# Expert steps of a fused attention and mixture-of-experts kernel: scatters behind the scaling, row loads ahead of the transposing transfers, another order in the first three steps

## The chip, the cores and the metric

The kernel runs on one core of one Trainium2 chip. The metric is the time of one execution on the device in microseconds (us); the kernel before has three timed runs, and one more execution was taken by the hardware profiler. Five engines work beside each other, each on its own list of instructions in the order of that list: PE (matmul), ACT (activations), DVE (vector), POOL (GpSimd) and SP, which only issues transfers. An engine that waits for one instruction starts none behind it.

## The reference

```python
def phi(x):                                   # x: q or k, scaled, [8, 8, 576, 64]
    proj = np.einsum('bhsd,md->bhsm', x, omega)
    h = proj - np.sum(x * x, -1, keepdims=True) / 2.0
    return np.exp(h - np.max(h, -1, keepdims=True)) / np.sqrt(m)
kv, z = einsum('bhsm,bhsd->bhmd', k_p, v), np.sum(k_p, axis=2)
num, den = einsum('bhsm,bhmd->bhsd', q_p, kv), einsum('bhsm,bhm->bhs', q_p, z) + 1e-06
x = (num / den).transpose(0, 2, 1, 3).reshape(4608, 512)
...
logits = xn @ en.T / tau                      # rows and expert embeddings, normalised
expert_idx = np.argmax(logits, axis=1)        # one of 8 experts for each token
gate_w = softmax(logits)[arange, expert_idx]
for e in range(8):
    mask = expert_idx == e
    h = np.maximum(x[mask] @ w1[e], 0.0)      # w1[e]: 512 x 1024
    out[mask] = gate_w[mask, None] * (h @ w2[e])   # w2[e]: 1024 x 512
```

Everything is float32. A product is made of three matmuls of parts rounded to fp32r (high by high, high by low, low by high).

## The kernel before

**Stages.** The attention runs over 36 tiles of 128 tokens and writes each token's 512 numbers, its logits and its number (a row of 521 floats) into a table `xs` in device memory, sorted by expert, with an indirect transfer. A small plan on DVE then says which 128 rows of `xs` and which quarter of which expert's weights each expert step takes. `NSTAT = 38` steps are written out; two of them (0 and 1) are worked off inside the attention, and the loop `for t in range(NPRE, NSTAT)` (L993, `NPRE = 2`) writes out steps 2 to 37.

**A step.** Step t takes 128 rows of `xs` (`xg[t]`, loaded by `x_of`, L852), multiplies them by the up weights w1 of its expert in two halves `pa` of 512 columns (24 matmuls of 128x128 by 128x512), applies the relu, turns the hidden words so that they can be the next stationary operand, multiplies by the down weights w2 (`down`, 24 matmuls into `nu`), scales with the gate (`scaled`, L247, DVE) and scatters the rows to `y` (`store`, L270, an indirect transfer that POOL issues). From step 5 on (`SHIFT = 5`) the down product at step t is that of u = t - 2, before that of u = t - 1. So the PE's list has 48 matmuls of 512 columns in each step of the steady part.

**Turning.** In the first steps `x_turned` and `h_turned` (L855, L877) transpose on PE. Otherwise the upper and lower 16 bits of each word go into two planes `pl` (`apart16`, L907: one plane by ACT, one by DVE), two transposing transfers on SP write `t16` (`turned16`, L912, shown as `t<-pl`), and `rejoin` (L924) puts the words `wd` together again; `summed` (L939) then makes the high parts (`xh`, `hh`, on ACT) and the low parts (`xl`, `hl`, on DVE). From `XPE = 9` on the rows of step t + 2 go through the same planes at step t, and the planes have one buffer each.

**Weights.** Step t uses a weight buffer of two halves of four quarters. `weights` (L988) loads 512 KB of one quarter into `raww1` or `raww2` (two buffers each) on SP, `split` (L897) rounds it: the first four quarters by ACT (high, L202) and DVE or POOL (low, L204), the later ones by DVE (high, L206) and POOL (low, L207). Steps 2 and 3 use a half that was filled during the attention; the matmuls of step t from 4 on wait for both parts of quarter t - 1.

**Loads of rows.** `xload` (L158) ties a load to earlier ones: up to t = 4 to the writes into `xs` (among them eight writes of padding, `pad`), later to the landing of the load before it (`last_x`). `ring` holds six buffers, so that the load for step t + 3 also waits until the scatter of step t - 3 has read its buffer.

All five engines' lists from L920 on stand as the code writes them (`manual_schedule`).

## Time and profile before

| | |
|---|---|
| median of three runs | 676.94 us (673.33 to 677.71) |
| the profiled execution | 671.0 us, of which the span of its instructions is 669.4 us |
| PE busy | 646.7 us (97%) |
| weight loads of PE | 541.1 us (81%) |
| DVE busy | 497.5 us (74%) |
| ACT busy | 416.0 us (62%) |
| POOL busy | 330.7 us (49%) |
| mean device memory traffic | 158 GB/s over the span |

The expert steps begin at about 247 us of the span and end with the last scatter at 662 us. A row of a timeline says at which us of the span an instruction starts, how many us it takes, its engine, its line, what it writes and reads (buffer numbers left out), and in brackets how long its engine sat idle before it and what ended that. A PE row's duration is longer than its share of the engine, since matmuls overlap: the distance from one start to the next counts. SP's rows (SPq) show the issue of a transfer, not its flight.

### The profile page before, as it was taken

How to read it: one execution, taken by the hardware profiler on the slowest of the kernel's cores; microseconds unless marked ns; L12 is line 12 of the kernel's file. 1: busy time of each engine (PE TensorE's matmuls, PEld its weight loads, DVE VectorE, ACT ScalarE, POOL GpSimd, SP SyncE). 2: the span in 40 equal slices, each digit the busy share in tenths (PEclk: the TensorE clock that was granted, in tenths of full speed). 3: DMA queues.
4: the chain of work that ended last, by engine and by line, in shares of the span. 5: the costliest groups of instructions: out<-in, count | busy, mean ns of one | idle time of the engine just before them, and what ended most of it. 6: DMA issues, size and time to landing. Idle time of an engine off the chain costs nothing. (4 is left out here: it accounts for less than half of the span.)

```text
span 669.4 us, 18009 instructions
## 1 busy us (share of the span) xinstructions
PE 646.7 (97%) x6051; PEld 541.1 (81%) x6052; DVE 497.5 (74%) x952; ACT 416.0 (62%) x1074; POOL 330.7 (49%) x414
## 2 busy tenths in 40 slices
PE   8999999999989998999999999999999999999993
PEld 7899999999877787788788778888888888888882
DVE  4688888899888745586878777777777777777871
ACT  6888898898886517553747465656565556565530
POOL 2013333435887544545555454655554655465553
PEclk9999999999999999999999999999999999999998
DMA  7546556569862268869887888787888787979721
GB/s 244 175 145 191 169 196 212 169 209 293 259 193 98 82 214 292 236 142 205 214 237 186 195 226 211 218 198 216 207 220 226 204 214 212 229 198 213 199 89 43
DMA packets 142346, 131.85 MB, mean 197 GB/s; under 512 B 106728, under 2 KB 106856, under 8 KB 142258
## 3 DMA queue, kind: packets, MB, share of 16 engines
q1 hardware_dynamic: 135794, 110.04, 61.3%
q0 software_dynamic: 6320, 20.38, 8.6%
q8 instruction: 55, 0.90, 0.6%
q10 hardware_dynamic: 144, 0.26, 0.1%
q14 instruction: 33, 0.27, 0.1%
HBM read 83.78 MB, written 21.97 MB: 158 GB/s over the span
## 5 line engine op out<-in xcount | busy, mean ns | idle before, releaser
L207 POOL TENSOR_TENSOR w1l<-raww,w1h 128x1024 f32 x34 | 89.8, 2641 | 164.4 <-DVE w1h L206 139.0
L241 PE MATMUL nu<-w2h,hl 128*128 (+1 forms) x288 | 113.7, 395 | 1.6 <-DVE hl L948 1.6
L241 PE MATMUL nu<-w2h,hh 128*128 (+1 forms) x288 | 113.8, 395 | 0.0
L241 PE MATMUL nu<-w2l,hh 128*128 (+1 forms) x288 | 113.6, 394 | 0.0
L241 PE MATMUL pa<-w1h,xl 128*128 (+1 forms) x280 | 111.1, 397 | 0.9 <-DVE xl L947 0.7
L241 PE MATMUL pa<-w1h,xh 128*128 (+1 forms) x280 | 110.8, 396 | 0.0
L241 PE MATMUL pa<-w1l,xh 128*128 (+1 forms) x280 | 110.5, 395 | 0.0
L905 DVE TENSOR_REDUCE wd<-t 128x1024 uint16<-128x1024 uint16 x68 | 90.0, 1323 | 3.4 <-DMA t<-pl 3.3
L338 ACT ACTIVATE ftk<-pjk,nmk 128x128 f32<-128x128 f32 x288 | 83.8, 415 | 5.7 <-DVE nmk L331 5.4
L338 ACT ACTIVATE ftq<-pjq,nmq 128x128 f32<-128x128 f32 x288 | 79.5, 418 | 9.5 <-DVE nmq L331 9.4
L909 ACT ACTIVATE pl<-pa 128x512 uint16<-128x512 uint16 x68 | 39.5, 586 | 72.2 <-DMA t<-pl 70.5
L905 DVE TENSOR_REDUCE pl<-pa 128x512 uint16<-128x512 uint16 x68 | 46.7, 690 | 49.7 <-ACT pl L909 49.6
L207 POOL TENSOR_TENSOR w2l<-raww,w2h 128x1024 f32 x34 | 83.0, 2442 | 0.0
L327 PE MATMUL pjq<-om,qt 64*128 64x128 f32 x576 | 76.2, 285 | 1.5 <-ACT ftk L338 1.0
L327 PE MATMUL pjk<-om,kt 64*128 64x128 f32 x576 | 76.3, 284 | 1.2 <-DVE om L600 1.2
L944 ACT ACTIVATE hh<-wd 128x1024 fp32r<-128x1024 f32 x34 | 36.1, 1061 | 59.9 <-DVE wd L905 52.5
L327 PEld LDWEIGHTS pjk<-om,kt 64*128 64x128 f32 x576 | 63.7, 187 | 8.7 <-issue 4.8
L241 PEld LDWEIGHTS nu<-w2h,hl 128*128 128x128 f32 x288 | 54.2, 188 | 14.7 <-DVE hl L948 2.1
L327 PEld LDWEIGHTS pjq<-om,qt 64*128 64x128 f32 x576 | 63.7, 187 | 2.8 <-ACT ftk L338 1.2
L241 PEld LDWEIGHTS pa<-w1h,xl 128*128 128x128 f32 x280 | 52.7, 188 | 15.1 <-DVE xl L947 2.9
L241 PEld LDWEIGHTS nu<-w2h,hh 128*128 128x128 f32 x288 | 54.3, 188 | 12.7
L241 PEld LDWEIGHTS nu<-w2l,hh 128*128 128x128 f32 x288 | 54.3, 188 | 12.5
(311 smaller groups left out, 1251.7 us busy)
## 6 DMA issues: line engine op xcount, KB each, us to landing
raww<-w1q SPq DMA_DIRECT2D x38, 512.0 KB, 4.1
raww<-w2q SPq DMA_DIRECT2D x38, 512.0 KB, 5.1
qt<-qT SPq DMA_DIRECT2D x36, 256.0 KB, 4.1
kt<-kT SPq DMA_DIRECT2D x35, 256.0 KB, 3.4
xgp<-xs SPq DMA_DIRECT2D x20, 260.5 KB, 3.1
xg<-xs SPq DMA_DIRECT2D x18, 260.5 KB, 3.2
rf<-w1q SPq DMA_DIRECT2D x4, 512.0 KB
rf<-w2q SPq DMA_DIRECT2D x4, 512.0 KB, 6.3
```

The source lines that it names most:

```text
L207: il = nc.gpsimd.tensor_tensor(at(l, dp), raw, at(h, dp).bitcast(F32), op=ALU.subtract)
L241: done.append(nc.tensor.matmul(dst, x[:, c * P : (c + 1) * P], ws.rearrange("p o f -> p (o f)"), start=(begin and i == 0 and k == 0), stop ...
L327: nc.tensor.matmul(st["pj" + w, i, a][:, c, :], st[w, i][r, c, :], om[r, :], start=True, stop=True)
L338: nc.scalar.activation(ft[:, h, :], pj[:, h, :], AF.Exp, bias=nm[:, h : h + 1])
L905: nc.vector.tensor_reduce(to, src.unsqueeze(2), axis=AX.X, op=ALU.max)
L909: nc.scalar.activation(planes[1][:, o : o + 512], halved(src)[:, :, 1], AF.Copy)
L944: nc.scalar.activation(hh, wd[:, 0:F], AF.Relu)
```

## The change

The change reorders; it adds and removes no work. In the loop over the steps:

- `store` follows each `scaled` at once, where it stood behind the two weight splits of the step.
- The load of the rows of step t + 3 (`rows_of`) stands ahead of the two transposing transfers of step t, where it stood at the step's end. Steps 2 and 5 keep it at the end.
- In the first three steps: the first two quarters of w1 are loaded ahead of those of w2; the load of step 4's rows goes ahead of the loads of w1's quarters 2 and 3; `h_turned` for step 2 stands in the middle of step 3's products; the splits of quarters 0 to 3 of w1 and w2 stand later in the lists; in step 4 `hl` is made ahead of the split of quarter 4.
- In step 5 the split of w1 stands ahead of the norms.

```diff
--- before.py
+++ after.py
@@ -884,15 +884,15 @@
     xg, xt, hid, raws, po = {}, {}, {}, {}, {}
     xg[NPRE] = xgp[NPRE]
     xg[NPRE + 1] = x_of(NPRE + 1, reg("row", NPRE + 1))
-    for t in range(NPRE):
-        for wn in W:
+    for wn in W:
+        for t in range(NPRE):
             raws[wn, t] = wload(wn, t, reg("wsrc", t))
     for e in range(PADP, E):
         pad(e)
     got.append(x2)
+    xg[NPRE + 2] = x_of(NPRE + 2, reg("row", NPRE + 2))
     raws["w1", NPRE] = wload("w1", NPRE, reg("wsrc", NPRE))
     raws["w1", NPRE + 1] = wload("w1", NPRE + 1, reg("wsrc", NPRE + 1))
-    xg[NPRE + 2] = x_of(NPRE + 2, reg("row", NPRE + 2))
 
     def split(wn, t):
         if t < NSTAT:
@@ -989,6 +989,10 @@
             if NPRE <= t < NSTAT and (wn, t) not in raws:
                 raws[wn, t] = wload(wn, t, reg("wsrc", t))
 
+        def rows_of(t):
+            if t < NSTAT and t not in xg:
+                xg[t] = x_of(t, reg("row", t))
+
         low, high, both = range(4), range(4, 8), range(8)
         for t in range(NPRE, NSTAT):
             u = t - 1 if t < SHIFT else t - 2
@@ -996,10 +1000,8 @@
             near = t in (NPRE, ends)
             if t > NPRE + 1:
                 weights("w1", t + 1)
-            if t > NPRE + 1:
+            if t > NPRE + 2:
                 weights("w2", u + 1)
-            elif t == NPRE:
-                weights("w2", t)
             late = (t - 1) in turn
             early = late and (t < SHIFT or t == ends)
             if early:
@@ -1012,6 +1014,8 @@
                     scaled(po.pop(v), xg[v], gates[v])
                     store(v, xg[v])
 
+            if t == SHIFT:
+                split("w1", t)
             if t == SHIFT - 1 or t > SHIFT and t % 3 == 0:
                 roots_of(batch(t)[0])
             elif t == SHIFT or t > SHIFT and t % 3 == 1:
@@ -1020,23 +1024,27 @@
             elif t > SHIFT:
                 inverted(totals[batch(t)[0] - 1])
             if t > SHIFT:
-                for v in po:
-                    scaled(po[v], xg[v], gates[v])
-            if t != NPRE + 1:
-                split("w1", t if t > NPRE else 0)
+                for v in list(po):
+                    scaled(po.pop(v), xg[v], gates[v])
+                    store(v, xg[v])
+            if early and t < SHIFT:
+                next(sm)
+            if t > NPRE + 1 and t != SHIFT:
+                split("w1", t)
             if t > SHIFT:
                 split("w2", u)
-                for v in list(po):
-                    po.pop(v)
-                    store(v, xg[v])
-            if early:
+            if early and t > SHIFT:
                 next(sm)
+            if t == NPRE + 2:
+                split("w2", NPRE)
             planes = None if near else [p2.tile([P, F + DM], U16, name=f"pl{t}_{k}", tag=f"pl{k}", bufs=1) for k in range(2)]
             par = reg("par", t) if t >= NQ else 0
             pa = [bank(f"pa{t}_{a}", ("px", "py")[a], 2) for a in range(2)]
             computed("w1", t, products(pa[0], xt[t], "w1", par, low, 0, True, True))
             if t == NPRE or NPRE + 1 < t < XPE - 1:
                 xt[t + 1] = x_turned(t + 1, xg[t + 1])
+            if t == NPRE + 1:
+                hid[t - 1] = h_turned(t - 1, h)
             if near:
                 h = words(t)
                 nc.scalar.activation(h[:, 0:512], pa[0], AF.Relu)
@@ -1055,7 +1063,11 @@
                 nc.scalar.activation(h[:, 512:F], pa[1], AF.Relu)
             else:
                 apart16(pa[1], planes, 512)
+                if t != SHIFT:
+                    rows_of(t + 3)
                 turn[t] = turned16(t, planes, F + DM if far else F)
+            if t == NPRE + 2:
+                weights("w2", u + 1)
             if late and not early:
                 rejoin(t - 1, wn[0], 0, F, 1)
             if t == SHIFT:
@@ -1068,19 +1080,19 @@
                 next(sm)
                 next(sm)
             if t == NPRE:
+                split("w1", 0)
                 split("w1", 1)
-                hid[t] = h_turned(t, h)
-                split("w2", 0)
-                split("w2", 1)
-                split("w1", t)
             elif t == NPRE + 1:
                 weights("w1", t + 1)
+                split("w1", NPRE)
                 split("w1", t)
                 down(u, low)
                 xt[t + 1] = x_turned(t + 1, xg[t + 1])
-                split("w2", u)
+                split("w2", 0)
+                split("w2", 1)
                 down(u, high)
-                weights("w2", u + 1)
+                weights("w2", NPRE)
+                weights("w2", t)
             elif t != SHIFT:
                 down(u, both)
             if t == NPRE + 1:
@@ -1089,8 +1101,7 @@
                 squares_of(NPRE + 3, NPRE + 4)
             elif NPRE + 2 < t < NSTAT - 2:
                 squares_of(t + 2)
-            if t + 3 < NSTAT:
-                xg[t + 3] = x_of(t + 3, reg("row", t + 3))
+            rows_of(t + 3)
         weights("w2", ends)
         split("w2", ends - 1)
         hid[ends] = h_turned(ends, h)
```

The first place is SP's list at the head of the expert steps. `raww_2` and `raww_3` with `w1q` are quarters 2 and 3 of w1; `xg_5122`, `xg_5123` and `xgp_103` are the rows of steps 4, 5 and 6; `t_3_0` and `t_3_1` are the transposing transfers of step 3. Before:

```order
L175 ISA
L175 DMA raww_2_5207<-w1q 128x1024
L175 ISA
L175 DMA raww_3_5209<-w1q 128x1024
L159 ISA
L159 DMA xg_5122<-xs 128x521
L175 ISA
L175 DMA raww_2_5214<-w2q 128x1024
L159 ISA
L159 DMA xg_5123<-xs 128x521
L916 DMA_TRANSPOSE t_3_0_5313<-pl_0_5281 128x8x128
L916 DMA_TRANSPOSE t_3_1_5315<-pl_1_5282 128x8x128
```

And of the change, in the same place, right behind the last write of padding:

```order
L159 ISA
L159 DMA xg_5122<-xs 128x521
L175 ISA
L175 DMA raww_2_5208<-w1q 128x1024
L175 ISA
L175 DMA raww_3_5210<-w1q 128x1024
L159 ISA
L159 DMA xg_5123<-xs 128x521
L159 ISA
L159 DMA xgp_103<-xs 128x521
L916 DMA_TRANSPOSE t_3_0_5306<-pl_0_5257 128x8x128
L916 DMA_TRANSPOSE t_3_1_5308<-pl_1_5258 128x8x128
```

The rows of step 4 moved ahead of the two weight quarters, the rows of step 6 moved from behind the transposing transfers to ahead of them, and the load of quarter 2 of w2 moved away behind them.

The second place is ACT's list at step 2. `raww_0` and `raww_1` are quarters of w1, `pt` and `ph` are transposes on PE, `wd` is the hidden words of step 2. Before:

```order
L202 ACTIVATE w1h<-raww_0_5191 128x1024
L228 ACTIVATE xh_5232<-pt_5234 128x512
L1042 ACTIVATE wd_5241<-pa_0_5218 128x512
L1055 ACTIVATE wd_5241<-pa_1_5219 128x512
L202 ACTIVATE w1h<-raww_1_5195 128x1024
L228 ACTIVATE hh_5258<-ph_0_5260 128x512
L228 ACTIVATE hh_5258<-ph_1_5267 128x512
```

And of the change:

```order
L228 ACTIVATE xh_5228<-pt_5230 128x512
L1050 ACTIVATE wd_5237<-pa_0_5214 128x512
L1063 ACTIVATE wd_5237<-pa_1_5215 128x512
L202 ACTIVATE w1h<-raww_0_5191 128x1024
L202 ACTIVATE w1h<-raww_1_5193 128x1024
L228 ACTIVATE hh_5273<-ph_0_5275 128x512
L228 ACTIVATE hh_5273<-ph_1_5282 128x512
```

The rounding of quarter 0 moved from ahead of the three activations of step 2 to behind them.

The third place is POOL's list at step 7, as in every step of the steady part: the low parts of one quarter of w1 and of w2, and the scatter to `y`. Before:

```order
L207 ISA
L207 TENSOR_TENSOR w1l<-raww_7_5639,w1h 128x1024
L207 ISA
L207 TENSOR_TENSOR w2l<-raww_5_5641,w2h 128x1024
L271 DMA y<-xg_5122 4608x512
```

And of the change:

```order
L271 DMA y<-xg_5122 4608x512
L207 ISA
L207 TENSOR_TENSOR w1l<-raww_7_5639,w1h 128x1024
L207 ISA
L207 TENSOR_TENSOR w2l<-raww_5_5641,w2h 128x1024
```

The scatter moved from behind the two low parts to ahead of them.

## Rows read from the trace of the kernel before

**Rows 1.** Busy time (instructions) by engine, granted clock, DMA share, GB/s; steady part
```profile
412.00:640.00 228.00, 228.00 (x982) 184.38 (x981) 174.49 (x254) 129.03 (x237) 121.73 (x61) 1.00 0.82 211
```

**Rows 2.** Timeline, PE: start, us, engine, line, operation, tiles, idle before; steps 2 to 5
```profile
254.98 1.15 PE L227 MATMUL ph<-ident,wd 128*128 128x128 f32 x8 [1.71 <-ACT wd L1042]
...
267.55 0.40 PE L241 MATMUL pa<-w1h,xh 128*128 x1
...
273.57 0.39 PE L241 MATMUL nu<-w2h,hh 128*128 128x512 f32 x1
...
275.85 0.50 PE L241 MATMUL nu<-w2h,hl 128*128 128x512 f32 x1 [1.65 <-DVE hl L948]
```

**Rows 3.** Timeline, PE, at the start of step 9
```profile
322.80 0.51 PE L241 MATMUL pa<-w1h,xl 128*128 x1 [0.73 <-DVE xl L947]
```

**Rows 4.** Waits from 240 us on: who, for whom, us in total, times, longest
```profile
ACT pl L909 <- DMA xg<-xs: 12.2, 14, 2.1
...
PEld pa L241 <- DVE xl L947: 2.9, 6, 1.2
```

**Rows 5.** Timeline, ACT, step 2
```profile
252.89 1.06 ACT L202 ACTIVATE w1h<-raww 128x1024 fp32r<-128x1024 f32 x1 [8.32 <-DMA raww<-w1q]
```

**Rows 6.** Timeline, DVE, steps 2 to 4
```profile
253.98 1.22 DVE L204 TENSOR_TENSOR w1l<-raww,w1h 128x1024 fp32r<-128x1024 f32 x1 [5.84 <-ACT w1h L202]
...
270.97 1.32 DVE L905 TENSOR_REDUCE wd<-t 128x1024 uint16<-128x1024 uint16 x1 [1.10 <-DMA t<-pl]
...
273.97 0.69 DVE L206 CAST w1h<-raww 128x1024 f32 x1 [1.67 <-DMA raww<-w1q]
274.58 1.22 DVE L948 SCALAR_TENSOR_TENSOR hl<-wd,hh 128x1024 fp32r<-128x1024 f32 x1
```

**Rows 7.** Timeline, SP (issues of transfers), steps 2 to 4
```profile
255.23 4.34 SPq L175 DMA_DIRECT2D raww<-w1q  x2
259.96 0.33 SPq L159 DMA_DIRECT2D xg<-xs  x1
...
264.68 2.76 SPq L916 DMA_TRANSPOSE t<-pl  x2
```

**Rows 8.** Line L175 at 248.3 us (quarter 1 of w2): issue to landing
```profile
DMA to landing us min/median/max: 9.8/9.8/9.8
```

**Rows 9.** Line L159 at 239.7 us (rows of step 2, alone): issue to landing
```profile
DMA to landing us min/median/max: 2.7/2.7/2.7
```

**Rows 10.** Line L175 at 259.2 us (quarter 3 of w1, alone): issue to landing
```profile
DMA to landing us min/median/max: 3.3/3.3/3.3
```

**Rows 11.** Line L916, step 3 (second transposing transfer): issue to landing
```profile
DMA to landing us min/median/max: 4.8/4.8/4.8
```

**Rows 12.** Line L916, 300 to 640 us (61 transposing transfers): issue to landing
```profile
DMA to landing us min/median/max: 3.7/4.1/6.2
```

**Rows 13.** Page, costliest groups: count, busy us, mean ns
```profile
L207 POOL TENSOR_TENSOR w1l<-raww,w1h 128x1024 f32 x34 | 89.8, 2641 | 164.4 <-DVE w1h L206 139.0
...
L207 POOL TENSOR_TENSOR w2l<-raww,w2h 128x1024 f32 x34 | 83.0, 2442 | 0.0
```

**Rows 14.** Timeline of all engines, one step of the steady part
```profile
404.11 0.74 DVE L248 TENSOR_SCALAR xgp<-nu,totalb 128x512 f32<-128x512 f32 x1
...
410.23 0.69 DVE L905 TENSOR_REDUCE pl<-pa 128x512 uint16<-128x512 uint16 x1 [0.49 <-ACT pl L909]
...
412.05 0.73 DVE L947 TENSOR_TENSOR xl<-wd,xh 128x512 fp32r<-128x512 f32 x1
412.06 0.99 POOL L271 DMA_INDIRECT y<-xgp  x1 [0.16 <-issue]
```

**Rows 15.** Line L271, 300 to 640 us (30 scatters): issue to landing
```profile
DMA to landing us min/median/max: 2.7/3.6/6.8
```

**Rows 16.** Timeline of all engines, step 6: a scatter beside a cast
```profile
292.44 1.08 POOL L271 DMA_INDIRECT y<-xg  x1 [0.30 <-issue]
...
292.58 0.69 DVE L206 CAST w1h<-raww 128x1024 f32 x1
```

## Prediction

> **What bounds the kernel now.** I read the busy times by stage first, to see who is never idle. In the steady part PE is busy in all of its 228 us, at the full granted clock, so a matmul costs 228.00 / 982 = 0.232 us [rows 1], and 48 of them make a step of 11.15 us. Nothing that only makes another engine faster or idle can shorten that part. So I asked the PE timeline for its idle places, and there are few in the expert steps. At 254.98 PE has waited 1.71 us for the hidden words of step 2; at 275.85 it has waited 1.65 us for `hl` of step 3 [rows 2]; at 322.80 it has lost 0.73 us to `xl` [rows 3]. PE's durations overlap, so such a number hides some 0.17 us of idle time each (a matmul shows about 0.40 and advances 0.232). For the short waits at other step starts the weight loads are the finer instrument: they waited for `xl` six times, 2.9 us in all [rows 4]. All that this change can win by removing waits is therefore 1.71 + 1.65 + 0.17 + 2.9 = 6.4 us, or 0.95% of the time, and that only if nothing new appears.
>
> Then the views of the engines behind these waits. ACT stood 8.32 us before 252.89 because its list had the rounding of a weight quarter that had not landed [rows 5]; `wd` of step 2 stood behind it, and PE behind that. For `hl`, DVE began the last join of the words at 270.97, when the transfer had landed, and ended at 272.29; ACT made `hh`, and then DVE waited for the landing of quarter 4 before it rounded it (273.97) and came to `hl` only at 274.58, to end at 275.80 [rows 6].
>
> **The change part by part.** No instruction is added or removed; what counts is order.
>
> *Step 2, ACT.* `wd` now stands ahead of the rounding, so PE does not wait at 254.98: 1.71 us gained, and PE would be ready for step 4 at 267.55 - 1.71 = 265.84 [rows 2].
>
> *SP at the head.* Here the change costs something. The load of step 4's rows must wait for every write into `xs`, and the last write of padding stands in SP's queue right behind quarter 1 of w2. That quarter was issued at 248.33 and landed 9.8 us later, at 258.1 [rows 8]; the load itself was issued without trouble at 259.96 [rows 7]. So the padding landed between 258.1 and 259.9; I take 259.0. In the change the two weight quarters stand behind this load on SP: quarter 2 is issued not at 255.23 but near 259.5, quarter 3 near 260.0 instead of at the end of the 4.34 us row, 259.24 [rows 7]. Rows alone take 2.7 us to land [rows 9], a quarter of twice the size 3.3 [rows 10], so each further 512 KB behind another costs about 2 x (3.3 - 2.7) = 1.2 us. Rows of step 4 land at 261.7, quarter 2 at 262.9, quarter 3 at 264.1. Rounding takes 1.06 on ACT [rows 5] and the low part 1.22 on DVE [rows 6]: quarter 3 is done at 264.1 + 1.06 + 1.22 = 266.4, and step 4's matmuls, which wait for it, start 0.55 late. `xl` of step 4 stands behind it on both engines, about 0.7 later; PE needs it two matmuls after the start, 0.46, so another 0.25 is lost. Step 4 gains 1.71 - 0.55 - 0.25 = 0.9.
>
> *The transposing transfers of step 3.* They now stand behind two loads of rows, and each load waits for the landing of the one before. Rows of step 5 are issued when those of step 4 landed (261.7), fly behind the quarters and land at 264.1 + 0.6 = 264.7. Only then are step 6's rows issued, and the two transposing transfers at 265.3 and, with 1.5 between, 266.8 (before: the first at 264.68 [rows 7]). The second took 4.8 us to land here [rows 11], the median of later ones is 4.1 [rows 12]; I take 4.4, so 271.2. Before, DVE started on it at 270.97. Behind it come 1.32 for joining, 1.06 for `hh`, 1.22 for `hl` and no cast between: `hl` ends at 274.8, against 275.80. PE, which reaches `hl` at 273.57 - 0.9 + 0.46 = 273.1, waits for it, and goes on **1.0 us earlier than before**. With the padding at 258.1 and 4.1 us of flight it is 2.1 earlier, with 259.9 and 4.8 it is 0.3 later.
>
> *POOL, steps 4 to 6.* Quarter 2 of w2 moved from an idle POOL into the row w1 quarter 4, w2 quarter 2, w2 quarter 3, w1 quarter 5. From the end of `hl` that is 0.69 + 2 x 2.64 + 2 x 2.44 = 10.85 us [rows 6, 13]. PE wants the last one after 22 matmuls (5.1) and step 5's 24 with their transposes (273.57 - 267.55 = 6.0 [rows 2]), at 11.1. It fits by 0.3 us; I count nothing, and up to 0.5 in the bounds. This is what is late next.
>
> *Later steps.* The scatter follows the scaling: POOL is idle there, so the scatter goes from 412.06 to about 404.11 + 0.74 + 0.1 = 404.95 [rows 14]. With the median flight of 3.6 us [rows 15] the buffer is free at 408.6, the rows can be issued then and land 2.7 later. ACT's waits for rows, 12.2 us in 14 of the steps [rows 4], 0.9 each, go, and with them most of what made `xl` late. Bounds: nothing won, or all 2.9. At step 9 PE lost 0.73 + 0.17 = 0.9; being 1.0 earlier eats much of that one again, since the planes and transfers ahead of it are set by DMA. I take **1.3**.
>
> *The tail* is untouched: the last scaling and scatter have nothing behind them in either list.
>
> Sum: 1.0 + 1.3 = 2.3 us. The profiled execution of 671.0 us would become 668.7. The median of the runs is 676.94, 5.9 above that execution, and the comparison goes by it: 676.94 - 2.3 = **674.6 us**.
>
> **The rivals.**
>
> *A. The new waits eat everything.* Padding at 259.9, flights of 4.8, the last weights of w1 0.5 late, and `xl` later still set by the transposing transfers: -0.3 - 0.5 + 0.8 = 0, so 677. For it: three loads chained landing to landing ahead of a transfer that PE waits for. Against: `hl` no longer stands behind a cast that waits for DMA.
>
> *B. Slower: SP is held by the scatter.* The transposing transfers of a step now stand behind a load that waits for a scatter's landing. They are ready when DVE's last plane is, at 410.23 + 0.69 = 410.92; the load can go at 404.95 + 3.6 + 0.4 for its issue = 409.0, 1.9 us ahead [rows 14, 15]. The point from which it decides is a flight of 5.5 us. At 6.8, the longest of 30, the transfers start 1.3 late; `xl` ended at 412.78, in time for the start of the next step by almost nothing. Were that usual, 29 steps with some 0.4 to 1.3 each give 12 to 38 us; at 0.4 it is 689. Against it: a median of 3.6, and that with scatters issued at 412.06, behind the planes' end and so beside the transposing transfers, which the new place is not.
>
> A scatter beside a cast took 1.08 us on POOL where 0.99 is usual, and the cast its normal 0.69 [rows 14, 16], so POOL and DVE don't hold each other up by more than 0.1 there. [...]
>
> *C. All waits go.* Padding at 258.1 and short flights: 2.1 + 2.9 = 5.0 us, so 671.9. For it: the transposing transfers no longer share the DMA engines with the scatter. Against: rows of w1's quarter 3 land later than before in any case.
>
> **How the numbers follow.** The forecast, a gain of 0.5 to 4, has 0.65; A 0.15; B 0.05; C 0.15. Without B the bounds are 671.9 and 677.4; the runs of before lie 3.6 below and 0.8 above their median, and a median of three can move by about half of that. That gives 669.8 to 678.6, with little beyond but B. About 1% (6.8 us) is what a measurement of this kernel can tell from no change. Faster by that needs C and a low draw of runs, 0.08; slower is B, 0.05; within it 0.87.
>
> **What would show it.** In the profile after: no wait of PE before `ph`; a wait of 0.3 to 1.5 us at the start of step 4 for quarter 3 of w1 or `xl`; a wait of 1 to 2 us before the matmuls with `hl` of step 3; SP's first two transposing transfers of step 3 at or after 265, behind two loads of rows; ACT's waits for rows gone; PE without idle time from step 10 on. The forecast is wrong if transposing transfers start late step after step (B), if the weight loads still wait for `xl` as often, or if the interval of matmuls in the steady part is no longer 0.232 us.

## The result, and the profile of the changed kernel

The changed kernel takes **681.41 us** (median of 6 runs, 680.06 to 682.87), the kernel before, on the same chip, 675.59 (6 runs, 673.33 to 677.71): a ratio of **1.0074**, 95% interval 1.0048 to 1.0099, or 3.2 to 6.7 us more. The forecast was 674.6, between 669.8 and 678.6; it started from 676.94, the median of the three runs that were there, which the three later runs brought down by 1.35.

The profiled execution of the changed kernel has 680.8 us, that of before 671.0. Most of these 9.8 us is not the change: step 2 starts at 254.62 in the one and at 247.20 in the other, though what is issued ahead of it is the same in both. Further traces show that this goes with the chip on which a trace was taken: on one chip step 2 starts near 248 and the kernel before has a median of 669.14 us, on three others it starts at 253 to 255 and that median is 675.4 to 675.8 (E9, E11, E12, E14, E15). So all traces are compared from their own first matmul of step 2; a step takes 11.15 us in some of them and 11.20 in others, which makes 1.4 us over the whole stretch and is told where it matters.

| us behind the first matmul of step 2 | before | after |
|---|---|---|
| step 4 could start (down(2) ends) | 20.35 | 18.39 |
| step 4 starts | 20.36 | 20.76 |
| PE goes on with `hl` of step 3 | 28.65 | 29.53 |
| step 5 starts | 33.87 | 34.75 |
| step 6 starts | 39.89 | 43.37 |
| last matmul | 411.46 | 413.62 |

Waits of PE in the first steps, changed kernel (who, for whom, us in total, times, longest):

```profile
PE pa L241 <- DVE xl L229: 2.5, 1, 2.5
PE pa L241 <- DVE w1l L204: 2.2, 1, 2.2
PE nu L241 <- DVE hl L948: 0.4, 1, 0.4
```

The wait for `ph` of [rows 2] is gone and that for `hl` is small. In their place stand two at the starts of steps 4 and 6. On PE's timeline (start, us, operation, tiles, idle before):

```profile
272.78 0.39 PE L241 MATMUL nu<-w2h,hl 128*128 128x512 f32 x1
275.38 0.47 PE L241 MATMUL pa<-w1h,xh 128*128 x1 [2.22 <-DVE w1l L204]
...
295.14 0.40 PE L241 MATMUL pa<-w1h,xl 128*128 x1
298.00 0.47 PE L241 MATMUL pa<-w1h,xh 128*128 x1 [2.46 <-DVE xl L229]
...
656.35 1.03 PE L227 MATMUL ph<-ident,wd 128*128 128x128 f32 x7 [0.32 <-ACT wd L1050]
```

From start to start less 0.23 they take 2.4 and 2.6 us, and the one at the last hidden words 0.5. By stretch (busy PE with its count, granted clock, DMA share, GB/s):

```profile
272.00:276.00 4.00, 1.78 (x9) 1.00 0.48 137
276.00:280.00 4.00, 4.00 (x13) 0.57 1.27 154
...
298.00:302.00 4.00, 4.00 (x20) 1.00 0.17 31
...
418.40:646.40 228.00, 228.00 (x983) 1.00 0.84 209
```

Behind the wait of step 4 the granted clock is at 0.5 for some 3.4 us (0.50 in all of 277 to 279): from 275.38 to 279.53 the matmuls advance 0.377 each in place of 0.234, 1.6 us more for 11 of them. Behind the wait of step 6 it stays at 1.00. The last line answers to [rows 1]: 0.232 us a matmul, as before.

Neither the wait of step 4 nor the half clock behind it lengthens the time, though. PE comes to `hl` of step 3 afterwards and has to wait for it in any case: `hl` ends 29.47 behind step 2's start, and step 5 starts 5.28 later. In the other traces in which step 4 waits (E2, E3, E6, E7 and the second one of the change in E9) `hl` ends at 29.06, 29.24, 29.80, 29.82 and 29.89, and step 5 starts 5.26 to 5.28 later in each, also in E2 and E3, where the clock stayed at 1.00. What counts up to step 5 is when `hl` ends; the wait of step 6 has nothing behind it that hides it.

SP in the head of the expert steps (answers to [rows 7]):

```profile
254.45 0.86 SPq L175 DMA_DIRECT2D raww<-w1q  x2
...
257.61 0.35 SPq L765 DMA_DIRECT2D xs<-w1l  x1
266.37 0.33 SPq L159 DMA_DIRECT2D xg<-xs  x1
266.94 0.91 SPq L175 DMA_DIRECT2D raww<-w1q  x2
269.01 0.33 SPq L159 DMA_DIRECT2D xg<-xs  x1
273.62 0.33 SPq L159 DMA_DIRECT2D xgp<-xs  x1
274.06 2.77 SPq L916 DMA_TRANSPOSE t<-pl  x2
```

SP's longest wait there, by its list of waits from 254 to 275:

```profile
SPq L159 <- DMA xs<-w1l: 8.1, 2, 7.1
```

SP stands from 257.96 to 266.37 at the load of step 4's rows, until the last write of padding (L765) has landed; w1's quarters 2 and 3 go only then, the transposing transfers of step 3 at 274.06, 19.4 behind step 2's start (17.5 before).

Step 5 on DVE, and in the last row the same sum of norms in a later step, with POOL idle:

```profile
287.12 0.68 DVE L905 TENSOR_REDUCE pl<-pa 128x512 uint16<-128x512 uint16 x1
287.72 2.88 DVE L206 CAST w1h<-raww 128x1024 f32 x1
...
290.72 2.16 DVE L970 TENSOR_TENSOR nrmb<-nrmb,n2b 128x3 f32<-128x3 f32 x1
292.92 2.32 DVE L971 TENSOR_TENSOR nrmb<-nrmb,roughb 128x3 f32<-128x3 f32 x1
...
297.16 0.69 DVE L229 TENSOR_TENSOR xl<-pt,xh 128x512 fp32r<-128x512 f32 x1 [1.51 <-ACT xh L228]
...
312.57 0.16 DVE L971 TENSOR_TENSOR nrmb<-nrmb,roughb 128x3 f32<-128x3 f32 x1
```

and on POOL and ACT:

```profile
285.29 2.41 POOL L207 TENSOR_TENSOR w1l<-raww,w1h 128x1024 f32 x1 [5.07 <-DVE w1h L206]
287.65 5.21 POOL L204 TENSOR_TENSOR w2l<-raww,w2h 128x1024 fp32r<-128x1024 f32 x2
292.83 2.39 POOL L207 TENSOR_TENSOR w1l<-raww,w1h 128x1024 f32 x1
...
295.68 0.30 ACT L261 ACTIVATE ex<-xgp,nrmb 128x8 f32<-128x8 f32 x1 [5.22 <-DVE nrmb L973]
```

A rounding that takes 0.69 us elsewhere [rows 6] takes 2.88, and a product and a sum of 3 columns take 2.16 and 2.32 in place of 0.16. The latter two end at 292.88 and 295.24, at the ends of POOL's subtractions (292.86 and 295.22). ACT waited 5.22 us for these norms; behind them stand its exps, `xh` and `xl` of step 6, and PE.

In the later steps, the weight loads' waits (first fence) and ACT's (second) from 310 on answer to [rows 4]:

```profile
PEld ph L227 <- ACT wd L1050: 0.8, 1, 0.8
```

```profile
ACT pl L909 <- PE pa L241: 50.4, 34, 4.2
```

No weight load waits for `xl` and ACT no longer waits for rows; it waits for PE, DVE and the transposing transfers.

### The profile page after: what moved, and what is told of

It is laid out like the page before. It is cut to its first block, busy times and chain, and to the rows that moved or that the text cites. A ratio compares the mean times of both kernels' runs of the same rounds, so it can differ in the third digit from the quotient of the medians.

```text
span 679.0 us, 18060 instructions
## 1 busy us (share of the span) xinstructions
PE 651.9 (96%) x6051; PEld 545.6 (80%) x6052; DVE 499.7 (74%) x952; ACT 417.3 (61%) x1074; POOL 326.1 (48%) x414
## 5 line engine op out<-in xcount | busy, mean ns | idle before, releaser
L207 POOL TENSOR_TENSOR w1l<-raww,w1h 128x1024 f32 x34 | 82.7, 2433 | 7.5 <-DVE w1h L206 5.1
L327 PE MATMUL pjk<-om,kt 64*128 64x128 f32 x576 | 77.8, 293 | 1.7 <-DVE om L600 1.7
L327 PEld LDWEIGHTS pjk<-om,kt 64*128 64x128 f32 x576 | 65.3, 195 | 9.2 <-issue 4.8
L241 PEld LDWEIGHTS pa<-w1h,xh 128*128 128x128 f32 x280 | 53.0, 189 | 17.6 <-issue 2.9
```

Of the source, the lines that this page charges most:

```text
L207: il = nc.gpsimd.tensor_tensor(at(l, dp), raw, at(h, dp).bitcast(F32), op=ALU.subtract)
L241: done.append(nc.tensor.matmul(dst, x[:, c * P : (c + 1) * P], ws.rearrange("p o f -> p (o f)"), start=(begin and i == 0 and k == 0), stop ...
L327: nc.tensor.matmul(st["pj" + w, i, a][:, c, :], st[w, i][r, c, :], om[r, :], start=True, stop=True)
```

## Experiments

Ratios are to the kernel before, run on the same chip with each group. "Stretch" is from the first matmul of step 2 to the last of all.

**E1, the steady half alone, on the kernel before.**

```
 if t > SHIFT:
     for v in list(po):
         scaled(po.pop(v), xg[v], gates[v])
         store(v, xg[v])
...
+if t > SHIFT: rows_of(t + 3)     # ahead of turned16; all else as before
```

> The kernel before with only the steady half of the change: the scatter directly behind the scaling, and rows loaded ahead of the transposing transfers, both from step 6 on; steps 2 to 5 and the first loads of weights stand as before. Measure: the stretch on PE from the first matmul of step 2 to the last matmul of all, 411.5 us before (247.20 to 658.66) and 413.6 after (254.62 to 668.25). Theory, that the two halves are independent and the steady half is good: the waits for xl from step 8 on go, the stretch is 409.4 to 409.9 (1.6 to 2.1 shorter), ACT no longer waits for rows, the time is 673.5 to 674.2. Rival 1, that the steady waits of before only follow from its first steps: stretch 411.5, time 675.6. Rival 2, that the steady half also lengthens what lies ahead of step 2 (that part took 7.4 us more in the profile after): step 2 starts at 252 or later instead of 247.2, time 677 or more.

Measured: 675.78 us, ratio 1.0011 (0.9996 to 1.0025); stretch 408.28. ACT's waits for rows are gone and no step loses time to `xl`, as in the theory. But the kernel is not faster: the shorter stretch is that of one execution, in which `hl` did not wait (in E15, the same kernel, it waited, and the stretch was 411.25 at 11.20 us a step).

**E2, the first steps alone:** the changed kernel with scatter and loads where they stood, from step 6 on.

> The kernel after with the steady half undone: scatter and loads of rows where they stood before, from step 6 on; steps 2 to 5 and the first loads of weights as in the change. Theory, that the reordered first steps are the loss: the new waits at the start of step 4 (2.6 us and a half clock behind it) and of step 6 (2.85) are there unchanged, the stretch from step 2 to the end is 415 to 416 (413.6 and 1.6 to 2.1 more), the time 682 to 684. Rival 1, that the steady half hurts and the first steps are neutral: stretch 411.5, time 675.6. Rival 2, that the lateness ahead of step 2 was chance of one execution: step 2 starts below 252, and the time is 678 to 680.

Measured: 680.69, ratio 1.0086 (1.0061 to 1.0111); stretch 414.0, waits of 2.2 at step 4, 1.6 before `hh` of step 3 and 2.8 at step 6 (start to start), the half clock not behind step 4 but behind step 6 (0.55 from 298 to 300). The first steps are the loss; the steady half is worth nothing that can be told from 1.0074. The time lies 1.3 under the theory's, which had credited the steady half with that.

**E3, the norms of step 5 ahead of the rounding again.**

```
-if t == SHIFT:
-    split("w1", t)
 ...norms_of, exps_of
-if t > NPRE + 1 and t != SHIFT:
+if t > NPRE + 1:
     split("w1", t)
```

> The kernel after with one move undone: in step 5 the rounding of w1's quarter 5 stands behind the norms and exps again, not ahead of them. Theory, that step 6 waits because DVE's rounding and its two small multiplies and adds for the norms were each held for as long as a subtraction of weights ran on POOL (2.88, 2.16 and 2.32 us instead of 0.69, 0.16 and 0.16), and the exps, xh and xl stand behind them: with the rounding out of the way the norms end near 38.3 us behind the first matmul of step 2 (41.0 in the change), xl of step 6 no longer ends last; the low part of quarter 5 does, behind two subtractions of w2, near 41.7; PE waits 0.9 to 1.4 us at the start of step 6 instead of 2.85, stretch 411.9 to 412.4. Rival, that step 6 waits for what arrives late from the first steps (rows, transposing transfers) or for exps however DVE is ordered: the wait stays 2.4 to 2.9 and the stretch 413.6.

Measured: 679.04, ratio 1.0056 (1.0040 to 1.0072); stretch 411.62, 0.3 under its bounds. PE's wait at step 6, start to start, is 1.01, and its releaser has changed, as the theory said:

```profile
PE pa L241 <- POOL w1l L207: 0.6, 1, 0.6
```

DVE was still held twice, the product for 2.14 and the sum for 2.33 us, but the norms end at 292.50, 38.0 behind step 2, with the rounding behind them:

```profile
289.76 2.33 DVE L971 TENSOR_TENSOR nrmb<-nrmb,roughb 128x3 f32<-128x3 f32 x1
...
292.44 0.69 DVE L206 CAST w1h<-raww 128x1024 f32 x1
```

**E4, step 4's rows behind w1's quarters again.**

```
-xg[NPRE + 2] = x_of(NPRE + 2, ...)
 raws["w1", NPRE] = wload(...)
 raws["w1", NPRE + 1] = wload(...)
+xg[NPRE + 2] = x_of(NPRE + 2, ...)
```

> The kernel after with one move undone: the load of step 4's rows stands behind w1's quarters 2 and 3 on SP again, so that these do not wait for the landing of the padding. Theory, that this load holds the quarters: they are issued near 9 and 10.3 us behind step 2's first matmul (12.3 and 12.9 in the change), step 4 starts without its wait of 2.6 and without the half clock behind it, 4 us earlier; but hl of step 3 hangs on the transposing transfers, which stay behind the chained loads of rows, so that most of it comes back as a longer wait for hl (0.8 becomes 3.5 to 5), and the stretch falls by only 0.3 to 1.2, to 412.4 to 413.3. Rival 1, that the wait for w1 was all the loss and hl follows from it: no wait for hl, stretch 409 to 409.8. Rival 2, that the quarters are late for another cause (flight beside others): step 4 waits as before, stretch 413.6.

Measured: 680.55, ratio 1.0067 (1.0048 to 1.0086). Step 4 starts at 19.10 without its wait, and the loss moves to `hl`, with the half clock now behind that wait (0.50 from 284 to 286):

```profile
PE nu L241 <- ACT hh L944: 2.6, 1, 2.6
```

The median is 0.07% or 0.5 us under the change's, less than the runs can tell apart. The stretch of its trace, 417.3, is 4 us over the theory. They were lost at the start of step 9 in that one execution (it has 684.4 us, the median 680.55), to the link of rival B. DVE, POOL and SP at step 8:

```profile
320.03 0.68 DVE L905 TENSOR_REDUCE pl<-pa 128x512 uint16<-128x512 uint16 x1
...
315.28 1.19 POOL L271 DMA_INDIRECT y<-xg  x1 [5.47 <-DVE xg L248]
...
322.51 0.33 SPq L159 DMA_DIRECT2D xg<-xs  x1
322.95 3.46 SPq L916 DMA_TRANSPOSE t<-pl  x2
```

The last plane was ready at 320.71, but the load of rows ahead of the transposing transfers waited for the landing of a scatter until 322.51, 7.2 us behind its issue, and the transfers started 2.2 behind the plane. At step 9 PE then lost 1.0 and 1.5 us to `xh` and `xl`, and the half clock behind them took 1.6 more.

**E10, the same, and in step 3 the rows of step 6 behind the transposing transfers** (`if t != SHIFT:` becomes `if t > SHIFT:` ahead of `rows_of`).

> The kernel after with two moves undone together: step 4's rows are loaded behind w1's quarters 2 and 3 again, and in step 3 the rows of step 6 behind the transposing transfers. The first move alone brought step 4 forward by 1.7 us with no wait there, and the wait for hl of step 3 grew from 0.8 to 3.0 with a half clock behind it. Theory, two locks in a row, padding and chained loads: now the transposing transfers go as soon as step 5's rows are issued, near 16 us behind step 2's first matmul (20.6 with the first move alone), hl ends near 25.6, PE waits for it 0 to 0.7, step 5 starts at 31 to 31.8 (34.75 in the change, 35.8 with the first move alone); the wait of step 6 stays, 2.5 to 2.9; stretch 409.8 to 410.6, time near 678. Rival, that the transposing transfers wait for the planes or fly longer for the quarters beside them: hl ends at 27.5 or later, PE waits 2 or more for it, step 5 starts at 33 or later, stretch 412 or more.

Measured: 679.51, ratio 1.0053 (1.0036 to 1.0071); stretch 412.40. The transposing transfers go at 16.0, PE waits 0.5 for `hl` and 0.2 for `hh`, step 5 starts at 31.92, 2.8 earlier than in the change. The wait of step 6 is there (2.83 from start to start), and this time the half clock behind it (0.50 from 296 to 298), 1.5 us that the expectation had not counted. Two locks in a row, as the theory had it.

**E11, only the last padding moved ahead of the weights.**

```
+for e in range(PADP, E):
+    pad(e)
 for wn in W:
     for t in range(NPRE):
         raws[wn, t] = wload(...)
-for e in range(PADP, E):
-    pad(e)
```

> The kernel after with one thing moved: the last write of padding is issued ahead of the four quarters of w1 and w2 that stood before it on SP, nothing else. Theory, that the head of the change hangs on the landing of this write behind 2 MB of weights: step 4's rows are issued 5.5 to 7.5 us behind step 2's first matmul (11.75 in the change), quarters 2 and 3 of w1 as soon as their buffers come free, near 9 and 10.3 (12.3 and 12.9), the transposing transfers of step 3 near 16 (19.4); step 4 starts near 18.6 to 19.1 without the wait of 2.6 (20.8), hl waits 0 to 0.8, step 5 starts at 31 to 32 (34.75); step 6 waits 2.5 to 2.9 as before, so the stretch is 410 to 411.5 and the time 677.5 to 679. Rival, that the rows wait for other writes (the padding that POOL issues, the scatters) or quarters for something else: the rows still go at 11 or later, step 4 waits 2 or more, stretch 413 to 414, time 681.

Measured: 671.31 on a chip where the kernel before takes 669.14, ratio **1.0017** (0.9992 to 1.0041). Step 2 starts at 247.65 here; SP:

```profile
246.20 0.35 SPq L765 DMA_DIRECT2D xs<-w1l  x1
...
251.91 0.34 SPq L159 DMA_DIRECT2D xg<-xs  x1
...
264.32 2.75 SPq L916 DMA_TRANSPOSE t<-pl  x2
```

Rows at 4.3 behind step 2 (11.75 in the change), transposing transfers at 16.7 (19.4), step 4 at 18.39, step 5 at 30.29. One wait of PE is left up to step 6, that for its `xl` (2.79 from start to start), with the half clock behind it (0.50 from 288 to 290); stretch 412.14 at 11.20 us a step, 410.7 at 11.155. So the padding alone was 0.57% of the time, 3.8 us, by the medians; each of the two ratios is known to some 0.25%, so this is 1.5 to 6 us. The ratio is better than the 1.003 to 1.005 that the expected time amounts to, within its interval.

**E7, both moves in step 5:** E3, and the low part of w2's quarter 3 on POOL behind that of w1's quarter 5. **E6, the second of them alone.**

```
-if NPRE + 1 < t < SHIFT:
-    split("w2", u)
 ...
     split("w1", t)
+if t == SHIFT:
+    split("w2", NPRE + 1)
```

> The kernel after with both moves in step 5: the norms ahead of the rounding of w1's quarter 5 on DVE, and w2's quarter 3 behind quarter 5 on POOL; the head and the chained loads as in the change. Theory: no wait at the start of step 6 (2.85 in the change, 1.0 with the norms alone), step 4 waits as before; the stretch from step 2 to the last matmul is 410.3 to 411.3 at 11.155 us a step (1.4 more at 11.20), 0.4 to 0.6% above the kernel before less 2.8 us, so a ratio of 1.002 to 1.0045. Rival, that the second product of step 4 now waits for w2's quarter 3: 0.5 us or more lost at 47 to 50 us behind step 2.

> The kernel after with one move: on POOL the low part of w2's quarter 3 stands behind that of w1's quarter 5, which so ends 2.4 us earlier; DVE's order (rounding, then norms) stays. Theory, that step 6 is set by DVE's chain, held once for each subtraction that POOL still has ahead or begins meanwhile: the rounding is held by w2's quarter 2, the norms by w1's quarter 5 and then by w2's quarter 3; the norms end as late as in the change, and PE waits 2.4 to 3.1 for xl at the start of step 6, though quarter 5 is there 2 us before. Rival, that quarter 5 on POOL sets the start: a wait of 0 to 0.8.

E7 measured: 677.94, ratio 1.0039 (1.0024 to 1.0053), 0.35% or 2.4 us under the change; step 6 starts 6.0 behind step 5, without a wait; step 4 waits as in the change; stretch 412.74 at 11.20 us a step, 411.3 at 11.155. E6: 681.53 in a single run; step 6 waits 1.78 from start to start, between the two expectations, and tells little: the move took w2's rounding on ACT along, which now stands between the exps and `xh` (`xh` starts at 295.31):

```profile
294.36 1.04 ACT L202 ACTIVATE w2h<-raww 128x1024 fp32r<-128x1024 f32 x1
```

Quarter 5 ended at 293.02, 2.2 before PE wanted it, so it did not set the start. The norms were held once less than in the change (the product took 0.16 us, the sum 2.34) and ended at 293.46, 2.2 earlier, which the theory had denied; what they alone would have cost there stays open.

**E13, both causes taken away:** E7 and E11 together, all loads in the order of the change.

> The changed kernel with both causes taken away and all its loads in its own order: the last write of padding ahead of the weights (step 5 started at 30.3 with it, against 33.0 to 34.3 before), and in step 5 the norms ahead of the rounding and w2's quarter 3 behind w1's quarter 5. Theory, that these two are the whole loss: no wait over 0.7 us from step 2 to the end but the last hidden words, step 6 starts at 36.2 to 36.6 (43.4 in the change, 39.0 to 40.3 before), stretch 406.6 to 408.2, which is 2 to 3.5 under the kernel before on the same chip: ratio 0.995 to 0.9975. Rival, that something of the change is left that costs time (the scatter's or the rows' new place, the lateness ahead of step 2): stretch as said, but a ratio of 0.999 or more; or a new wait takes the place, stretch 409 or more.

Measured: **674.06**, ratio **0.9983** (0.9971 to 0.9996). PE's waits in the first steps:

```profile
PE nu L241 <- DVE hl L948: 0.5, 1, 0.5
PE nu L241 <- ACT hh L944: 0.2, 1, 0.2
```

Stretch 408.9 at 11.20 us a step, 407.4 at 11.15, as expected; step 6 at 37.28, 0.7 later than expected, by these two waits. The ratio lies between the theory's 0.995 to 0.9975 and the rival's 0.999, and its interval reaches both. It is under 1: with its two losses repaired the change beats the kernel before, by 1.2 us (0.3 to 2.0). Whether the kernel before would gain from the early padding too was not tried; in E12, with the loads in the order of before, it gained nothing.

**E8 and E12, other repairs:** E7 and E10 together; and the padding of E11 as well.

> The kernel after with four moves altered: step 4's rows behind w1's quarters 2 and 3, step 6's rows behind the transposing transfers of step 3, the norms of step 5 ahead of the rounding of w1's quarter 5 on DVE, and the low part of w2's quarter 3 behind that of w1's quarter 5 on POOL. Theory: as with the first two moves, and without the wait of step 6: of the two subtractions of w2 that held DVE's norms only one is left ahead, and the low part of quarter 5 ends 2.4 earlier than with the norms moved alone, where step 6 waited 1.0 for it: stretch 407 to 408, the time 674.5 to 676. Compared with the kernel before with the steady half alone (stretch 408.3, 675.8) this is the gain of 1.7 at step 2's hidden words less what the padding costs. Rival 1, that the two repairs overlap (an earlier step 5 wants quarter 5 earlier, so step 6 still waits 1 us or more): stretch 409 or more, 677. Rival 2, that w2's quarter 3 is now late for the second product of step 4: a wait for w2l at step 6's second product, stretch 408.5 or more.

> The version with the four moves altered (stretch 409.1 at 11.20 us a step, which is 407.6 at 11.155; 675.75 measured), and the last write of padding ahead of the weights as well. Theory: step 4's rows come early, so the wait of 0.8 for them at their transposes goes, and hl of step 3 ends earlier: stretch 406 to 407 at 11.155 us a step, 407.5 to 408.5 at 11.20; time 674 to 675.2. Rival, that the quarters now land later by the padding's place, or that hl is set by what stands beside it: no change, 675.5 to 676.

Measured: E8 675.75, ratio 1.0000 (0.9984 to 1.0017), stretch 409.08 at 11.20 as expected; E12 669.44, ratio 0.9998 (0.9978 to 1.0018), stretch 409.44 at 11.20, so the padding adds nothing once the rows stand behind the quarters (its rival). In both PE waits 0.3 to 0.7 for step 4's rows to land. With the padding early, the order of the change (E13) is the better one.

**E9, E14, E15, the two kernels and E1 again.**

> The kernel before once more, for a second trace. The first one shows an execution of 671.0 us where the median is 675.5; step 2 starts at 247.20 in it, and at 253.4 to 254.6 in the five traces of changed kernels, though the instructions and waits ahead of step 2 read the same in all of them. Theory, chance: the first execution was early ahead of step 2, and this one starts step 2 at 250 to 255, with a stretch of 408 to 412 behind it. Rival, a fixed effect of the change on what lies ahead of it (the place of the code, say): step 2 starts at 246 to 249 again.

> The changed kernel once more, for a second trace. Theory: step 2 starts at 250 to 255; the waits at the start of step 4 (2.2 to 2.8) and of step 6 (2.6 to 3.0) are there again, since both follow from the order; stretch from step 2 to the last matmul 413 to 415. Rival, that the two waits were one execution's: at least one is under 1 us, stretch 411.5 or less.

> The kernel before a third time. The two traces so far differ in three places: step 2 starts at 247.20 or 254.74, hl of step 3 was late for the landing of a quarter (first) or held beside a subtraction on POOL (second), and xl was late in the later steps only in the first. Theory, that these are chance of an execution and the first start was rare: step 2 starts at 252 to 255; no lost time from step 8 on, that is 11.15 to 11.20 a step, so that the steady half of the change had nothing to win; hl waits 0 to 2.3. Rival, that the later steps usually lose 1.3 to 2 us to xl: starts of steps 8 to 11 are 11.3 or more apart in the mean.

> The kernel before with the steady half of the change alone, a second time. Its first trace had a stretch of 408.3, 2.5 to 3.2 under the two of before, and its median was that of before. Theory, that the difference was the wait for hl of step 3 (none in that execution, 1.9 and 2.3 in those of before), which the steady half does not touch: this time hl waits 0 to 2.3, by chance, steps from 8 on are 11.15 to 11.20 apart. Rival, that the steady half removes it: no wait for hl again, stretch 408 to 408.6.

Measured: step 2 starts at 254.74 and 248.23 in the kernel before, 254.37 in the changed one, 247.45 in E15; E14 and E15 ran on one chip, both E9 on another. The lateness ahead of step 2 is not of the change; the rival "a fixed effect" falls, and so does the expectation that the third trace of before would start it at 252 to 255. The changed kernel shows both waits again (2.81 and 2.82 from start to start). The kernel before in its second trace:

```profile
PE nu L241 <- DVE hl L948: 2.1, 1, 2.1
PE ph L227 <- ACT wd L1042: 1.7, 1, 1.7
```

and in its third:

```profile
PE ph L227 <- ACT wd L1042: 1.3, 1, 1.3
PE nu L241 <- DVE hl L948: 0.5, 1, 0.5
```

The weight loads waited 2.9 us for `xl` in the first trace [rows 4], 0.2 in the second and not at all in the third. With the first steps of before, step 5 starts at 33.87, 34.32 and 33.00, and with the same first steps in E1 and E15 at 32.03 and 33.54: its wait for `hl` is anything from none to 2.3. In the second trace that wait has another cause than in the first; DVE and POOL:

```profile
280.63 3.15 DVE L948 SCALAR_TENSOR_TENSOR hl<-wd,hh 128x1024 fp32r<-128x1024 f32 x1 [0.45 <-ACT hh L944]
...
280.32 2.38 POOL L207 TENSOR_TENSOR w1l<-raww,w1h 128x1024 f32 x1 [3.78 <-DVE w1h L206]
```

`hl` took 3.15 in place of 1.22, beside a subtraction on POOL that ended at 282.70.

## Why the prediction was wrong, step by step

*Which steps failed.* Three terms of the sum. The landing of the loads behind the padding was priced too low, and with it the start of the transposing transfers: PE went on with `hl` of step 3 0.9 us later than before where 1.0 earlier was forecast, 1.9 us. The row of subtractions on POOL in steps 4 to 6 was counted as nothing, and step 6 came 2.6 us late, since DVE was held beside them. The 1.3 us to be won in the later steps were not there. That is 5.8 of the 7.3 us between the forecast of 2.3 less and the measured 5.0 more; 0.5 are the last hidden words, and for the other 1.0 no run names a cause. The kernel before itself differs by more from one execution to the next: its wait for `hl` is anything from none to 2.3 us.

*Do the accounts close?* Against before, the change costs 0.74%. Removing the padding's hold gives 0.57% (E11), removing DVE's in step 5 0.35% (E7), both 0.91% (E13). Each of these is a difference of two ratios from different chips and known to some 0.3%, so that the sum comes out to 0.01 is luck. The stretches of the traces, at 11.155 us a step, are 2.9, 2.3 and 6.2 us under the change's, the first with a half clock of 1.5 behind step 6 that the change does not have there; so they close to within 1 us. Without these two the change is worth -0.17%, 1.2 us, half of the 2.3 forecast.

*Step 2, ACT: right.* PE did not wait for `ph`, and would have been ready for step 4 at 18.39, 1.97 earlier than before (1.71 forecast).

*SP at the head: the mechanism right, a term of the sum too small.* The forecast had the rows of step 4 waiting for the padding until 11.8 behind step 2; it was 11.75. It had them land at 14.5; the next load went at 14.4. Then it failed: "each further 512 KB behind another costs about 2 x (3.3 - 2.7) = 1.2 us". Quarter 2 was rounded on ACT at 16.5 (forecast landing 15.7), and quarter 3's low part, forecast to end at 19.2, ended at 20.6. Step 4 lost 2.4 in place of 0.8. The price came from the difference between two transfers, each alone in its place, with twice the size between them; the rounding of quarter 3 started 1.8 behind that of quarter 2, on ACT, which stood waiting for its landing both times. That the difference of size and place is what made the price too low is argued, not tested.

*The half clock had no term, and needed none at step 4.* The trace of before gave no reason for one: behind its waits of 2.1 and 2.0 (start to start) the clock stayed at 1.00. In the change its 1.6 us are hidden behind `hl`, as E2 and E3 show; in E2, E10 and E11 it falls behind the wait of step 6, where nothing hides it.

*The transposing transfers of step 3: wrong by the same term.* They went at 19.4 in place of 18.1, since step 5's rows landed behind both quarters, and DVE started on the second one 4.9 behind its issue in place of 4.4. PE went on with `hl` 0.9 later than before, not 1.0 earlier. E10 and E11 bring the transfers to 16.0 and 16.7, and the wait is then 0.5 or none.

*POOL, steps 4 to 6: the number right, the wrong link.* "It fits by 0.3 us": the last subtraction was forecast 10.85 behind the end of `hl`, and ended 11.1 behind it, at 295.22, 0.15 before PE wanted it. What was overlooked is what these subtractions do to DVE. The profile of before had it: its norms in step 5, on DVE and then POOL,

```profile
278.11 2.33 DVE L971 TENSOR_TENSOR nrmb<-nrmb,roughb 128x3 f32<-128x3 f32 x1
...
278.02 2.40 POOL L204 TENSOR_TENSOR w2l<-raww,w2h 128x1024 fp32r<-128x1024 f32 x1
```

show one addition of 3 columns held for 2.33, behind a single subtraction; in its other two traces the product ahead of it took 1.42 and 2.38. The change filled that place of POOL with two more, and put a rounding ahead of the norms, so three DVE instructions were each held, and step 6 came 2.6 late. The prediction had looked only at a scatter of POOL beside a cast of DVE, where it found neither more than 0.1 us longer [rows 14, 16]. Which instructions were held the rows show: 2.88, 2.16 and 2.32 for the rounding, the product and the sum; but 0.68 for the reduction at 287.12 and 0.69 for the subtraction that makes `xl` of step 5 at 285.92, both beside a subtraction on POOL that ran from 285.29 to 287.70. Why the former and not the latter, no run shows.

*Later steps: the mechanism right, the gain not there.* ACT's waits for rows and the weight loads' waits for `xl` went, as forecast. But the 2.9 us of [rows 4], of which 1.3 were to be won, were one execution's; the second and third traces of before have 0.2 and none. The step that failed is to price a stall of the steady part from one execution. E1 shows the result: 1.0011. That the changed trace gains these 1.3 us from step 6 on against the first trace of before is luck in the choice of that trace.

*The tail: not untouched.* The scatter ahead of the last step's subtractions put both of them beside the last `hl`. On DVE and POOL, and in the last row the same `hl` before:

```profile
649.39 6.21 DVE L948 SCALAR_TENSOR_TENSOR hl<-wd,hh 128x1024 fp32r<-128x1024 f32 x1
...
649.77 2.40 POOL L207 TENSOR_TENSOR w1l<-raww,w1h 128x1024 f32 x1
652.13 2.39 POOL L207 TENSOR_TENSOR w2l<-raww,w2h 128x1024 f32 x1
...
641.71 3.42 DVE L948 SCALAR_TENSOR_TENSOR hl<-wd,hh 128x1024 fp32r<-128x1024 f32 x1
```

6.21 in place of the 3.42 that all three traces of before have there (1.22 in the steps ahead of it), and ACT's words behind it: 0.5 us of PE at the end, in every trace that has the steady half.

*Rivals.* A named the right direction, new waits that eat the gain. It had the last weights of w1 0.5 late, where step 4 waited 2.4, and PE at `hl` of step 3 0.3 later than before, where it was 0.9; the 2.6 at step 6 it had not at all. C did not come: even with both losses repaired (E13) the gain is 1.2 us, not 5.0.

B was put aside too lightly. Its link is there in the change; SP's waits from 310 to 640 us:

```profile
SPq L159 <- DMA y<-xg: 70.4, 14, 6.2
```

with as much again for `y<-xgp` (62.4 us in 14 loads), against 10.2 and 8.5 before. The scatters' median flight is 5.8 us, over the 5.5 at which B decides, where 3.6 was taken from the old place. In 19 of 25 steps of the steady part the transposing transfers start right behind the load of rows, up to 1.4 us behind the last plane, where before it was never more than 0.03. In this trace PE lost nothing by it, so the forecast was right about the price, but not for its reason; in E4's trace it cost 4 us in one step. How often that happens the runs do not tell: E1, which has the same order in the steady part, is not slower than before by more than 0.25%. The scatter itself takes a little longer on POOL where it now stands, a median of 1182 ns where 0.99 us was usual [rows 14].

*The range.* Its ends do not follow from what was said of them: half of 3.6 and of 0.8 beside 671.9 and 677.4 gives 670.1 to 677.8, not 669.8 to 678.6. The result lies outside of either.

## What to carry to other kernels

When a change fills an idle place of POOL, ask not only whether POOL is done in time but which DVE instructions fall beside it: here the rounding and the product and the sum of 3 columns, beside subtractions of 2.4 us, took 2.88, 2.16 and 2.32 us in place of 0.69, 0.16 and 0.16, while a reduction beside one took its 0.68. Before a load is moved ahead of others in a queue, find what its wait hangs on and how much traffic is ahead of that; moving the small write that it waited for was worth 0.57% here (known to some 0.35%), where the reorder with its losses repaired gave 0.17%. Before a wait is priced, ask what the engine would wait for next: the 2.4 us of step 4 and the half clock behind them cost nothing, because `hl` came later still. Price a short stall of a steady loop from more than one execution.

## What the runs showed of the hardware

Between step 2 and the last matmul the granted clock fell to 0.5 nine times in 8 of 17 traces, for some 3.4 us each. Eight times it fell at a place where PE had started no matmul for 2.57 to 3.01 us. The ninth, in E4 at step 9, stands behind gaps of 1.20 and 1.69 us between starts, with two matmuls between them. Other single gaps, up to 2.49, left it at 1.00. It was not every gap of the longer kind either: the second one of the changed kernel, 2.85 and 2.82 in its two traces, some 23 us behind the first, left the clock at 1.00, while gaps of 2.79 to 2.83 at the same place halved it in E2, E10 and E11, where no gap that halved it had come before.

How long DVE was held differed: at 649.39 `hl` stood through both of POOL's subtractions (6.21), while the rounding at 287.72 ran between two of them, which together took 5.21 in place of 2 x 2.41 (the first row of POOL in step 5 has 2.41 for one).
